# Weight conversion of a folded attention and two-layer network: sign bit through a leaky activation, half of layer two's weight sums by accumulating DMAs, four operand sets instead of five

## The chip, the cores and the metric

The kernel runs on one core of a Trainium2 chip. The metric is the device time of one execution in microseconds (us); less is better. TensorE (PE) does the matrix products, VectorE (DVE) and ScalarE (ACT) work on rows of 128 partitions, GpSimd (POOL) and SyncE (SP) issue DMAs here; a DMA that adds to its target is issued from POOL.

## What is computed

```python
def _attn_ref(q, k, v, tau):
    qn = q / (np.linalg.norm(q, axis=1, keepdims=True) + 1e-06)
    kn = k / (np.linalg.norm(k, axis=1, keepdims=True) + 1e-06)
    s = kn.transpose(0, 2, 1) @ qn / tau
    a = softmax(s)                      # 256 x 256
    return v @ a
def _moe_ref(x, w_in, w_out):           # layer 1
    h = x @ w_in
    return (h * (1.0 / (1.0 + np.exp(-1.702 * h)))) @ w_out
def _moe2_ref(x, w_in, w_out):          # layer 2
    h = x @ w_in
    return np.maximum(0.01 * h, h) @ w_out
```

There are 6016 tokens, 256 channels and 2048 hidden columns. The attention is one over channels, so its 256x256 matrix is multiplied into layer one's first weights once (the "fold"), and the tokens of `v` go straight into layer one. The four weight matrices arrive as 64-bit floats.

## The kernel before

**Number format.** Each 32-bit operand is split into a rounded high part and a low part (the rest), and each product is three matmuls: high by high, low by high, high by low (`terms`, line 96). ACT usually makes the high part with a copy, DVE the low part with a subtraction.

**Work.** The tokens are six pairs of blocks of 512 (the last pair 448), the hidden columns eight pairs of 128, numbered f. A pass i is one layer for one pair of token blocks: passes 0 to 5 are layer one, 6 to 11 layer two. Pass 0 (`hidden_first`) multiplies the plain way; passes 1 to 3 (`step`) use a Strassen scheme of seven products in place of eight for the first matrix of a layer; passes 4 to 11 (`strassen_step`) use it for both. The scheme multiplies sums of weight blocks by sums of token blocks. A step is one f of one pass. In a step of passes 1 to 3 PE does seven first products in the order A11, S2, A12, S3, S1, S4, A22, into two PSUM banks, and between them eight products with the second weights for the step before (`put`).

**Weight preparation.** For each of the 32 pieces of 128x512 values, `convert` (layer one, pass 0) or `words_of` (layer two, passes 1 to 3) makes 32-bit floats of the two words of each 64-bit one: ACT multiplies the high words, read as floats, by a power of two (`scale_words`, 212), DVE shifts the low word (line 242), joins the sign bit to it (247) and then the shifted high word (251). For layer two's pieces, keys `w2i` and `w2o`, one key is begun in each step by `begin_next` at its end. Then three closures follow:

- In the next step `run_casts`, after product S3, lets ACT make the high part of the plain blocks (375 and 376 for `w2i`, where two blocks are also negated; 301 for `w2o`), and the scaling of the key after that.
- At the end of that step `run_due` runs `second`: DVE makes the low part, SP stores both, and DVE makes the four block sums in place (`combine`, 198).
- In the step after that, `run_casts` begins with the high part of the sums (406, "rest" in what follows), and `close`, between DVE's low part of g11 (1140) and its sum into `cc` (1151), runs `third`: low part, store.

The buffer `ta` of a piece is one of two, and so are the buffers `ws` of the split blocks. DVE's sum into `cc` reads the PSUM bank that the next step's first product A11 writes.

**Layer one's sums** (`sums_first`) are made from the folded first weights and the second weights, which take a way through DRAM (`raw1`), eight DVE operations of 128x128 for each f. While `ahead` is set, in pass 0, DVE makes their high parts, later ACT.

**Strassen steps.** Each needs three sets of two buffers for the second products' token operands (`operands`, 1177): g0 in its own step, g1 and g2 in the next one. There are five sets, four of them in the buffers of layer one's second weights and one in `gs`.

Of the kernel before, what the change touches and what calls it, by code (L numbers as in the profile page):

```python
# [7 lines left out]
F32 = mybir.dt.float32  # L8
# [9 lines left out]
def tile_kernel(  # L18
# [28 lines left out]
    nc = tc.nc  # L47
# [32 lines left out]
    x2 = [dram.tile([P, 4, w], F32, name=f"x2{p}") for p, w in enumerate(width)]  # L80
    raw1 = [dram.tile([P, 2, 4, P], F32, name=f"raw1{f}") for f in range(NF)]
    w2a = [dram.tile([P, 7, 2, P], F32, name=f"w2a{f}") for f in range(NF)]
# [44 lines left out]
    with tc.manual_schedule():  # L127
# [28 lines left out]
        def load_piece(key):  # L156
            name, f = key
            if name == "both":
                t = raws[key] = early.tile([P, 2, 4, P], F32, tag="cv", name="cb", bufs=3)
                nc.sync.dma_start(out=t, in_=raw1[f])  # L160
                return
# [35 lines left out]

        def combine(a, turned=False):

            (minus_sum if turned else add)(a[:, 2], a[:, 3], a[:, 2])  # L200
            yield
            subtract(a[:, 3], a[:, 0], a[:, 3])
            yield
            if turned:
                minus_sum(a[:, 0], a[:, 2], a[:, 0])
            else:
                subtract(a[:, 0], a[:, 2], a[:, 0])
            yield
            subtract(a[:, 1], a[:, 1], a[:, 0])
            yield  # L210

        def scale_words(t):

            h = t[:, :, :, 1].bitcast(F32)
            nc.scalar.activation(out=h, in_=h, func=AF.Copy, scale=2.0 ** -112)

# [20 lines left out]
        def bits(key):  # L237

            t = raws[key]
            b = t[:, :, :, 1]  # L240
            a = early.tile([P, 4, P], I32, tag="ta", name="ta", bufs=2)
            nc.vector.tensor_scalar(
                out=a, in0=t[:, :, :, 0], scalar1=29, scalar2=7,
                op0=ALU.logical_shift_right, op1=ALU.bitwise_and,
            )
            yield
            nc.vector.scalar_tensor_tensor(  # L247
                out=a, in0=b, scalar=-0x80000000, in1=a, op0=ALU.bitwise_and, op1=ALU.bitwise_or
            )
            yield  # L250
            nc.vector.scalar_tensor_tensor(
                out=a, in0=b, scalar=3, in1=a, op0=ALU.logical_shift_left, op1=ALU.bitwise_or
            )
            raws.pop(key)
            to_convert.remove(key)
            next_load()
            words_out[key] = a.bitcast(F32)

        def convert(key):
# [10 lines left out]
            if name == "wo":  # L270
                hi, lo = (wo[f][:, s].rearrange("p k c -> p (k c)") for s in range(2))
                for j in range(2):
                    nc.sync.dma_start(
                        out=raw1[f][:, 1, 0::3] if j == 0 else raw1[f][:, 1, 1:3],
                        in_=a[:, 2 * j:2 * j + 2],
                    )
# [26 lines left out]
        def sums_first(f):  # L303
# [9 lines left out]

            yield from combine(t[:, 0])
            high(lambda: wa[f][:, 3:, 0], t[:, 0])
            yield from combine(t[:, 1])
            high(out_blocks, t[:, 1])

            def second():
                subtract(wa[f][:, 3:, 1], t[:, 0], wa[f][:, 3:, 0].bitcast(F32))  # L320
# [3 lines left out]
                subtract(x[:, :, 1], t[:, 1], x[:, :, 0].bitcast(F32))  # L324
                nc.sync.dma_start(out=w1o[f][:, 2:6], in_=x.bitcast(F32))
# [14 lines left out]
        def words_of(key):  # L340
# [30 lines left out]

            if name == "w2i":
                def both_bases():
                    x = kept["x"] = new_blocks(name)
                    nc.scalar.copy(x[:, 0, 0], a[:, 0])
                    nc.scalar.activation(
                        out=x[:, 1:3, 0], in_=a[:, 1:3], func=AF.Copy, scale=-1.0
                    )
                casts.append(both_bases)
            else:  # L380
                high(base_blocks, a[:, some])

            def second():
                x = kept["x"]
                if name == "w2i":
                    subtract(x[:, 0, 1], a[:, 0], x[:, 0, 0].bitcast(F32))
                    minus_sum(x[:, 1:3, 1], a[:, 1:3], x[:, 1:3, 0].bitcast(F32))
                else:
                    subtract(x[:, some, 1], a[:, some], x[:, some, 0].bitcast(F32))
                if name == "w2i":  # L390
                    nc.sync.dma_start(out=dst[:, :3], in_=x[:, :3].bitcast(F32))
                else:
# [23 lines left out]

            due.append(second)

# [359 lines left out]
        fold_half(raw0, 0, 1)  # L778
        nc.sync.dma_start(out=raw1[0][:, 0], in_=raw0)
        folded.add(0)  # L780
# [5 lines left out]
        def fold(f):  # L786
# [11 lines left out]
            nc.sync.dma_start(out=raw1[f][:, 0], in_=raw)  # L798
            folded.add(f)
# [417 lines left out]
        def strassen_step(i, f):  # L1217
# [51 lines left out]
            def first_stage():  # L1269
# [5 lines left out]
                hook("first")  # L1275
                subtract(t13, g[:, 1:3], g[:, 0:2])
                nc.scalar.copy(g1[0], t13)  # L1277
                subtract(t24[:, 0], g[:, 2], t13[:, 0])
                subtract(t24[:, 1], g21, t24[:, 0])
                subtract(g1[1], t13, g1[0].bitcast(F32))  # L1280
# [36 lines left out]
        def begin_drain(i):  # L1317
# [40 lines left out]
            def part_two():  # L1358
                if i == LAST:
                    return  # L1360
                add(to["c"], to["c"], sums[i, M5])
                add(tb, ta, sums[i, M7])

            def join():
                burst(other)
                if i == LAST:
                    add(ta, ta, sums[i, M6])
                    add(tb, ta, sums[i, M7])
                    add(ta, ta, sums[i, M5])
# [62 lines left out]
        def place_v(i, n):  # L1432
            nc.vector.transpose(out=staged_x[i][:, n], in_=vblocks_in.pop(n))

        def cast(to, i, n, j):
            nc.scalar.copy(to[:, 0, n, :width[i % NPAIR]], staged_x[i][:, j])

        def low(to, i, n, j):
            w = width[i % NPAIR]
            subtract(to[:, 1, n, :w], staged_x[i][:, j], to[:, 0, n, :w].bitcast(F32))  # L1440

# [218 lines left out]
```

## Time and profile before

| | us |
|---|---|
| median of 3 runs (lowest, highest) | 1006.01 (1005.89, 1007.33) |
| the profiled execution's own time | 1006.63 |
| its span, first to last instruction | 1004.9 |
| TensorE's granted clock in it, share of full speed | 0.999 |
| PE busy | 997.7 (99%) |
| DVE busy | 881.5 (88%) |
| ACT busy | 760.8 (76%) |
| POOL busy | 21.8 (2%) |
| data moved | 208.36 MB, mean 207 GB/s |

The profiled execution took 1.7 us more than its span, and 0.6 us more than the median. A busy PE is not a PE at its peak, as a matmul's end is modelled; idle time of an engine that others do not wait for costs nothing. In rows of the timeline and the chain the first number is the start in us from the span's start.

### The profile page before, as it was taken

Reading aid. Unit: us, or ns where it says so; the run is one execution under the profiler, and the core shown is the slowest. Engines: PE = TensorE matmul, PEld = TensorE weight load, DVE = VectorE, ACT = ScalarE, POOL = GpSimd, SP = SyncE. Lnnn points to the kernel's source line nnn. Section 1 sums busy time; section 2 is a strip of 40 time slices with the busy share of each in tenths; the row PEclk is TensorE's granted clock in tenths of the full one; section 3 lists DMA queues with packets and bytes.
Section 4 is the critical chain, followed back from the end, with each engine's and each line's share of the span. In section 5 each row is a group of like instructions: output and inputs, shape, how many; then the busy total and the mean of one; then the engine's idle time right before and its main releaser. Section 6 shows DMA issues by size and latency. Waiting matters only on the chain.

```text
span 1004.9 us, 13108 instructions
## 1 busy us (share of the span) xinstructions
PE 997.7 (99%) x4448; PEld 824.6 (82%) x4448; DVE 881.5 (88%) x1304; ACT 760.8 (76%) x1221; POOL 21.8 (2%) x31
## 2 busy tenths in 40 slices
PE   9999999999999999999999999999999999999998
PEld 8888887887888888877998887887887887788897
DVE  7899977878887887999898998998998998998986
ACT  7775557787878787886887886886886897797683
POOL 0000000000000000000000000000000000000000
PEclk9999999999999999999999999999999999999999
DMA  9866477745546753764976775875875875785662
GB/s 347 271 178 183 153 236 247 249 174 189 158 152 195 228 177 84 255 211 139 308 242 218 263 227 168 240 237 180 248 225 193 219 234 188 211 260 178 177 205 48
DMA packets 161619, 208.36 MB, mean 207 GB/s; under 512 B 100624, under 2 KB 126736, under 8 KB 160400
## 3 DMA queue, kind: packets, MB, share of 16 engines
q1 hardware_dynamic: 153808, 200.38, 61.4%
q0 software_dynamic: 3456, 6.16, 3.7%
q10 hardware_dynamic: 4288, 0.98, 0.5%
q8 instruction: 35, 0.57, 0.2%
q14 instruction: 32, 0.26, 0.1%
HBM read 161.87 MB, written 45.61 MB: 206 GB/s over the span
## 4 chain that ended last, share of the span: by engine, by line
PE 97%; DMA 1%; DVE 1%; issue 0%; ACT 0%; ACTq 0%; SPq 0%; DVEq 0%
PE h L100 53%; PE y L841 18%; PE y L100 17%; PE y L1340 5%; PE y L565 3%; DMA qk<-in_k_dram 1%; PE h L712 1%; PE h L841 0%; PE y L712 0%; DVE cc L107 0%; ACTq L498 0%; PE y L670 0%; DVE ta L107 0%; PE h L585 0%; DVE ta L247 0%
## 5 line engine op out<-in xcount | busy, mean ns | idle before, releaser
L100 PE MATMUL h<-xa,wi 128*128 128x512 f32 (+1 forms) x765 | 201.9, 385 | 0.0
L100 PE MATMUL y<-g,wo 128*128 128x512 f32 (+1 forms) x744 | 198.5, 389 | 0.4 <-issue 0.4
L100 PEld LDWEIGHTS h<-xa,wi 128*128 128x128 f32 x765 | 141.5, 188 | 29.7 <-ACT tv L1233 3.3
L100 PEld LDWEIGHTS y<-g,wo 128*128 128x128 f32 x744 | 139.6, 188 | 29.2 <-issue 4.5
L100 PE MATMUL h<-xb,wi 128*128 128x512 f32 (+1 forms) x573 | 152.8, 391 | 0.0
L107 DVE TENSOR_TENSOR g<-t,g 128x1024 fp32r<-128x1024 f32 (+1 forms) x124 | 147.4, 1189 | 0.0
L100 PEld LDWEIGHTS h<-xb,wi 128*128 128x128 f32 x573 | 106.9, 188 | 24.5 <-issue 3.2
L841 PE MATMUL y<-gd,wo 128*128 128x512 f32 (+1 forms) x498 | 124.2, 388 | 0.0
L841 PEld LDWEIGHTS y<-gd,wo 128*128 128x128 f32 x498 | 93.1, 188 | 18.7
L100 PE MATMUL h<-xa,wa 128*128 128x512 f32 x384 | 104.2, 390 | 0.1
L100 PE MATMUL h<-g,wo 128*128 128x512 f32 (+1 forms) x372 | 102.7, 384 | 0.0
L811 ACT ACTIVATE g<-g 128x512 f32<-128x512 f32 (+1 forms) x92 | 57.8, 628 | 44.3 <-DVE g L107 43.3
L100 PE MATMUL h<-xb,wa 128*128 128x512 f32 x312 | 83.9, 391 | 0.7 <-DVE xb L104 0.5
L100 PEld LDWEIGHTS h<-xa,wa 128*128 128x128 f32 x384 | 71.5, 188 | 15.4 <-DVE cc L107 0.5
L100 PEld LDWEIGHTS h<-g,wo 128*128 128x128 f32 x372 | 69.8, 188 | 12.7
L841 PE MATMUL y<-g,wo 128*128 128x512 f32 (+1 forms) x297 | 79.1, 388 | 0.0
L1277 ACT CAST g<-t 128x1024 fp32r<-128x1024 f32 (+1 forms) x62 | 63.8, 1029 | 19.5 <-DVE t L107 18.3
L107 DVE TENSOR_TENSOR g<-g,g 128x1024 fp32r<-128x1024 f32 (+1 forms) x62 | 73.9, 1192 | 0.3
L107 DVE TENSOR_TENSOR t<-g 128x1024 f32<-128x1024 f32 (+1 forms) x62 | 73.2, 1181 | 0.0
L100 PEld LDWEIGHTS h<-xb,wa 128*128 128x128 f32 x312 | 58.3, 188 | 14.0 <-DVE xb L104 1.0
L107 DVE TENSOR_TENSOR g<-tt,h 128x512 f32<-128x512 f32 (+1 forms) x62 | 41.7, 672 | 31.2 <-ACT tt L1241 26.9
L1248 ACT CAST g<-g 128x1024 fp32r<-128x1024 f32 (+1 forms) x62 | 63.7, 1027 | 2.0
(192 smaller groups left out, 1525.6 us busy)
## 6 DMA issues: line engine op xcount, KB each, us to landing
wi<-w2a SPq DMA_DIRECT2D x48, 896.0 KB, 5.5
wo<-w2o SPq DMA_DIRECT2D x46, 768.0 KB, 4.2
wi<-w1a SPq DMA_DIRECT2D x16, 896.0 KB, 6.3
wo<-w1o SPq DMA_DIRECT2D x16, 768.0 KB, 4.8
cv<-in_moe_w_in_dram SPq DMA_DIRECT2D x32, 256.0 KB, 3.4
w1a<-wa SPq DMA_DIRECT2D x8, 896.0 KB, 3.6
stg<-x SPq DMA_DIRECT2D x5, 1024.0 KB, 4.8
stg<-x POOLq DMA_DIRECT2D x20, 256.0 KB, 4.3
```

The source lines that it names most:

```text
L100: nc.tensor.matmul(dst, lhsT=w, rhs=x, start=start, stop=stop, skip_group_check=more)
L107: nc.vector.tensor_tensor(out=out, in0=in0, in1=in1, op=op)
L565: nc.tensor.matmul(s_ps[h][:, :C], lhsT=t[:, 1, r, h * P:(h + 1) * P], rhs=t[:, 0, r, :], start=(j == 0 and r == 0), stop=(j == last and r ...
L712: nc.tensor.matmul(pw, lhsT=e[:, d, c0], rhs=wi[:, x, d], start=i == 0, stop=i == len(todo) - 1)
L811: nc.scalar.activation(out=out, in_=in_, func=AF.Prelu, alpha=0.01)
L841: nc.tensor.matmul(ys[key][kc], lhsT=ws[x], rhs=y, start=first and n == 0, stop=closing or (final and n == 2), skip_group_check=closing,)
L1248: nc.scalar.copy(g0[0], g[:, 0::2])
L1277: nc.scalar.copy(g1[0], t13)
L1340: nc.tensor.matmul(sums[i, M1], lhsT=x, rhs=y, start=False, stop=True, skip_group_check=True,)
```

## The change

- **Sign bit.** ACT's scaling becomes a leaky activation with slope 2^32 for negative values: their exponent then has a bit that DVE's shift by three moves into the sign. DVE's operation of line 247 goes, for all 32 pieces.
- **Pass 0.** The high parts of the first weights (line 284) and of the folded ones (796) go from DVE to ACT. `raw1` has another layout, so that layer one's sums are four operations of 128x256 instead of eight of 128x128.
- **Layer two's sums.** Signs are turned so that `w2i`'s plain blocks are no longer negated; the token operands B21, T4 and T2 of layer two and some of its sums get the other sign instead, in operations that were there before. Of the four sums DVE makes two; the other two are DMAs from POOL that add one 128x128 block of `ta` to another, the second of them reading what the first wrote.
- **Order.** `second` now runs in `close`, before DVE's sum into `cc`; `rest` stays in the next step's `run_casts` and reads what the DMAs added; `third` runs in that step's `run_due`.
- **Operand sets.** Four instead of five.

```diff
         def scale_words(t):
             h = t[:, :, :, 1].bitcast(F32)
-            nc.scalar.activation(out=h, in_=h, func=AF.Copy, scale=2.0 ** -112)
+            nc.scalar.activation(out=h, in_=h, func=AF.Prelu, scale=2.0 ** -112, alpha=2.0 ** 32)
...
-            nc.vector.scalar_tensor_tensor(
-                out=a, in0=b, scalar=-0x80000000, in1=a, op0=ALU.bitwise_and, op1=ALU.bitwise_or
-            )
             yield
...
-                (nc.scalar.copy if f == 0 else nc.vector.tensor_copy)(wi[:, 0], flat)
+                nc.scalar.copy(wi[:, 0], flat)
...
-            yield from combine(t[:, 0])
-            high(lambda: wa[f][:, 3:, 0], t[:, 0])
-            yield from combine(t[:, 1])
-            high(out_blocks, t[:, 1])
+            yield from combine(t)
+            high(lambda: wa[f][:, 3:, 0], t[:, :, 0])
+            high(out_blocks, t[:, :, 1])
...
-                for _ in combine(a, name == "w2i"):
-                    pass
-                casts.insert(0, lambda: nc.scalar.copy(rest_blocks(), a))
-                closing.append(third)
+                minus_sum(a[:, 2], a[:, 3], a[:, 2])
+                subtract(a[:, 3], a[:, 0], a[:, 3])
+                for to, n in ((0, 2), (1, 0)):
+                    nc.gpsimd.dma_start(out=a[:, to], in_=a[:, n], accum_op=ALU.add)
+                casts.insert(0, rest)
+
+            def rest():
+                nc.scalar.copy(rest_blocks(), a)
+                due.append(third)
...
-            due.append(second)
+            closing.append(second)
...
-            nc.vector.tensor_copy(hi, raw)
+            nc.scalar.copy(hi, raw)
             subtract(lo, raw, hi.bitcast(F32))
...
-        sets = [(4 - 3 * (NF * (LAST - FIRST) + REST - 1)) % 5]
+        sets = [0]
         def operands(name):
-            i = sets[0] % 5
+            i = sets[0] % 4
             sets[0] += 1
-            if i == 4:
-                return [late.tile([P, 2, BLK], F32R, tag="gs", name=name, bufs=2) for _ in range(2)]
...
+                if layer == 1:
+                    subtract(t13, g[:, 1:3], g[:, 0:2])
+                    nc.scalar.copy(g1[0], t13)
+                    subtract(t24[:, 0], g[:, 2], t13[:, 0])
+                    subtract(t24[:, 1], g21, t24[:, 0])
+                else:
+                    subtract(t13, g[:, 0:2], g[:, 1:3])
+                    nc.scalar.copy(g1[0], t13)
+                    minus_sum(t24[:, 0], t13[:, 0], g[:, 2])
+                    add(t24[:, 1], g21, t24[:, 0])
```

How DVE's work stands in a step of passes 1 to 3 that finishes a `w2i` key's plain blocks; before, from the end of `close` on (`ta` is the piece, `cv` the words of the next key):

```order
L107 TENSOR_TENSOR w2os<-ta,w2os 128x4x128
L107 TENSOR_TENSOR cc<-tv,h_2408 128x512
L107 TENSOR_TENSOR g_2452<-tt,g_2452 128x512
L107 TENSOR_TENSOR w2i<-ta,w2i 128x128
L113 SCALAR_TENSOR_TENSOR w2i<-ta,w2i 128x2x128
L113 SCALAR_TENSOR_TENSOR ta<-ta 128x128
L107 TENSOR_TENSOR ta<-ta 128x128
L113 SCALAR_TENSOR_TENSOR ta<-ta 128x128
L107 TENSOR_TENSOR ta<-ta 128x128
L242 TENSOR_SCALAR ta<-cv 128x512
L247 SCALAR_TENSOR_TENSOR ta<-cv,ta 128x512
L251 SCALAR_TENSOR_TENSOR ta<-cv,ta 128x512
```

And now, from the low part of g11 on:

```order
L107 TENSOR_TENSOR g_2432<-tp,g_2432 128x512
L107 TENSOR_TENSOR w2i<-ta,w2i 128x3x128
L113 SCALAR_TENSOR_TENSOR ta<-ta 128x128
L107 TENSOR_TENSOR ta<-ta 128x128
L107 TENSOR_TENSOR cc<-tv,h_2390 128x512
L107 TENSOR_TENSOR g_2433<-tt,g_2433 128x512
L107 TENSOR_TENSOR w2os<-ta,w2os 128x4x128
L239 TENSOR_SCALAR ta<-cv 128x512
L245 SCALAR_TENSOR_TENSOR ta<-cv,ta 128x512
```

The key's low part and two sums stand ahead of `cc` now, where the earlier key's low part of the sums (`w2os`) stood, and that one has gone behind g22; five operations for a `w2i` key have gone, four for a `w2o` one.

ACT in the middle of such a step, before: `rest` of the earlier key, the scaling, the plain blocks of a `w2i` key, then the high part of g11 (`g_2637`) and what follows it.

```order
L1131 COPY tt<-h_2595 128x512
L406 CAST w2os<-ta 128x4x128
L215 ACTIVATE cv<-cv 128x512
L375 CAST w2i<-ta 128x128
L376 ACTIVATE w2i<-ta 128x2x128
L1139 CAST g_2637<-tp 128x512
```

And now (g11 is `g_2432`):

```order
L1116 COPY tt<-h_2391 128x512
L391 CAST w2os<-ta 128x4x128
L212 ACTIVATE cv<-cv 128x512
L295 CAST w2i<-ta 128x3x128
L1124 CAST g_2432<-tp 128x512
```

`rest` has kept its place ahead of g11; two operations for a `w2i` key's plain blocks have become one. POOL, which had issued nothing in passes 1 to 3, now stands so (the rows before are the same without the third):

```order
masks.py:199 ISA
masks.py:199 AFFINE_SELECT ident<-ident 128x128
L387 DMA ta<-ta 128x128 x32
L1484 DMA stg<-x_65 128x512 x4
L1484 DMA stg<-x_66 128x512 x4
```

32 accumulating DMAs, two for each of 16 keys, have come ahead of layer two's; PE's order is the same in both kernels.

## Rows read from the trace of the kernel before

**Rows 1.** The profile's first part: busy us, share of the span, by engine.

```profile
PE 997.7 (99%) x4448; PEld 824.6 (82%) x4448; DVE 881.5 (88%) x1304; ACT 760.8 (76%) x1221; POOL 21.8 (2%) x31
```

**Rows 2.** The chain that ended last: share of the span by engine.

```profile
PE 97%; DMA 1%; DVE 1%; issue 0%; ACT 0%; ACTq 0%; SPq 0%; DVEq 0%
```

**Rows 3.** Windows: 25 us of pass 0, busy us by engine, clock.

```profile
100.00:125.00 25.00, 25.00 (x123) 21.14 (x122) 24.21 (x45) 13.59 (x22) 0.00 (x0) 1.00 0.51 158
```

**Rows 4.** Waits of PE, 54 to 400 us: in total, times, longest.

```profile
PE h L100 <- DVE xb L104: 0.5, 1, 0.5
...
PE h L100 <- DVE tt L107: 0.2, 1, 0.2
```

**Rows 5.** Tile `ta` (a piece's 32-bit words): duration in ns, least/median/most.

```profile
L247 DVE SCALAR_TENSOR_TENSOR ta<-cv,ta x32: 681/693/696, 42.4 to 371.8; 128x512 int32<-128x512 int32 x32
...
L107 DVE TENSOR_TENSOR ta<-ta x48: 286/292/294, 214.8 to 380.3; 128x128 f32<-128x128 f32 x48
...
L113 DVE SCALAR_TENSOR_TENSOR ta<-ta x16: 291/293/294, 214.5 to 370.2; 128x128 f32<-128x128 f32 x16
...
L284 DVE CAST wi<-ta x7: 422/427/429, 57.7 to 109.2; 128x512 fp32r<-128x512 f32 x7
```

**Rows 6.** Tile `cv`: ACT's scaling, in ns least/median/most.

```profile
L215 ACT ACTIVATE cv<-cv x32: 657/670/702, 38.2 to 364.8; 128x512 f32<-128x512 f32 x32
```

**Rows 7.** The page's costliest groups: layer two's leaky activation (busy us, mean ns).

```profile
L811 ACT ACTIVATE g<-g 128x512 f32<-128x512 f32 (+1 forms) x92 | 57.8, 628 | 44.3 <-DVE g L107 43.3
```

**Rows 8.** The chain in order of time: start, us, what; in pass 4.

```profile
410.91 3.40 PE h L100 x15
```

**Rows 9.** Timeline where passes 1 and 2 meet: start, us, [idle before].

```profile
228.35 1.89 DVE L104 TENSOR_TENSOR xb<-stg,xb 128x512 fp32r<-128x512 f32 x3
...
229.09 0.50 PE L100 MATMUL h<-xb,wa 128*128 128x512 f32 x1 [0.53 <-DVE xb L104]
...
239.32 0.32 SPq L880 DMA_DIRECT2D x<-stg  x1
```

**Rows 10.** Timeline of one step of pass 2, and the next step's rest.

```profile
262.10 0.62 ACT L406 CAST w2is<-ta 128x512 fp32r<-128x512 f32 x1
...
263.18 0.52 ACT L301 CAST w2o<-ta 128x384 fp32r<-128x384 f32 x1
...
264.25 0.69 DVE L107 TENSOR_TENSOR g<-tp,g 128x512 fp32r<-128x512 f32 x1 [1.08 <-ACT g L1139]
...
264.86 0.69 DVE L107 TENSOR_TENSOR w2is<-ta,w2is 128x512 fp32r<-128x512 f32 x1
...
265.46 0.68 DVE L107 TENSOR_TENSOR cc<-tv,h 128x512 f32<-128x512 f32 x1
...
266.66 0.55 DVE L107 TENSOR_TENSOR w2o<-ta,w2o 128x384 fp32r<-128x384 f32 x1
...
266.85 0.84 PE L100 MATMUL h<-xa,wa 128*128 128x512 f32 x3
...
267.25 1.27 DVE L107 TENSOR_TENSOR ta<-ta 128x128 f32<-128x128 f32 x4
...
272.30 0.62 ACT L406 CAST w2os<-ta 128x512 fp32r<-128x512 f32 x1
```

**Rows 11.** DMA issues: times, KB each, median us to landing.

```profile
stg<-x POOLq DMA_DIRECT2D x20, 256.0 KB, 4.3
...
x<-stg SPq DMA_DIRECT2D x4, 1024.0 KB, 4.7
...
w2o<-w2o SPq DMA_DIRECT2D x10, 256.0 KB, 2.4
...
w2r<-wr SPq DMA_DIRECT2D x4, 64.0 KB, 2.1
```

**Rows 12.** POOL's accumulating DMAs of passes 7 to 11 (tile `stg`).

```profile
L1487 POOL DMA_DIRECT2D stg<-x x24: 865/865/1013, 490.9 to 907.1; - x24
...
DMA to landing us min/median/max: 3.6/4.3/8.4
```

More of the change, by code (lines that the diff above doesn't have):

```diff
@@ L80, in tile_kernel @@
     x2 = [dram.tile([P, 4, w], F32, name=f"x2{p}") for p, w in enumerate(width)]
-    raw1 = [dram.tile([P, 2, 4, P], F32, name=f"raw1{f}") for f in range(NF)]
+    raw1 = [dram.tile([P, 4, 2, P], F32, name=f"raw1{f}") for f in range(NF)]
     w2a = [dram.tile([P, 7, 2, P], F32, name=f"w2a{f}") for f in range(NF)]
@@ L158, in load_piece @@
             if name == "both":
-                t = raws[key] = early.tile([P, 2, 4, P], F32, tag="cv", name="cb", bufs=3)
+                t = raws[key] = early.tile([P, 4, 2, P], F32, tag="cv", name="cb", bufs=3)
                 nc.sync.dma_start(out=t, in_=raw1[f])
@@ L196, in next_load, with combine @@
                     return
-        def combine(a, turned=False):
-            (minus_sum if turned else add)(a[:, 2], a[:, 3], a[:, 2])
+        def combine(a):
+            add(a[:, 2], a[:, 3], a[:, 2])
             yield
@@ L203, in combine @@
             yield
[L204 to L207, printed above, removed]
+            subtract(a[:, 0], a[:, 2], a[:, 0])
             yield
@@ L273, in convert @@
                     nc.sync.dma_start(
-                        out=raw1[f][:, 1, 0::3] if j == 0 else raw1[f][:, 1, 1:3],
+                        out=raw1[f][:, 0::3, 1] if j == 0 else raw1[f][:, 1:3, 1],
                         in_=a[:, 2 * j:2 * j + 2],
@@ L312, in out_blocks @@
                 return kept["x"][:, :, 0]
-            yield from combine(t[:, 0])
-            high(lambda: wa[f][:, 3:, 0], t[:, 0])
-            yield from combine(t[:, 1])
-            high(out_blocks, t[:, 1])
+            yield from combine(t)
+            high(lambda: wa[f][:, 3:, 0], t[:, :, 0])
+            high(out_blocks, t[:, :, 1])
             def second():
-                subtract(wa[f][:, 3:, 1], t[:, 0], wa[f][:, 3:, 0].bitcast(F32))
+                subtract(wa[f][:, 3:, 1], t[:, :, 0], wa[f][:, 3:, 0].bitcast(F32))
                 combined.add(f)
@@ L323, in second @@
                 x = kept["x"]
-                subtract(x[:, :, 1], t[:, 1], x[:, :, 0].bitcast(F32))
+                subtract(x[:, :, 1], t[:, :, 1], x[:, :, 0].bitcast(F32))
                 nc.sync.dma_start(out=w1o[f][:, 2:6], in_=x.bitcast(F32))
@@ L370, in rest_blocks @@
                 return kept["y"][:, :, 0]
[L372 to L381, printed above, removed]
+            high(base_blocks, a[:, some])
             def second():
                 x = kept["x"]
[L385 to L389, printed above, removed]
+                subtract(x[:, some, 1], a[:, some], x[:, some, 0].bitcast(F32))
                 if name == "w2i":
@@ L778, in tile_kernel @@
         fold_half(raw0, 0, 1)
-        nc.sync.dma_start(out=raw1[0][:, 0], in_=raw0)
+        nc.sync.dma_start(out=raw1[0][:, :, 0], in_=raw0)
         folded.add(0)
@@ L795, in fold @@
             hi, lo = wa[f][:, :4, 0], wa[f][:, :4, 1]
-            nc.vector.tensor_copy(hi, raw)
+            nc.scalar.copy(hi, raw)
             subtract(lo, raw, hi.bitcast(F32))
-            nc.sync.dma_start(out=raw1[f][:, 0], in_=raw)
+            nc.sync.dma_start(out=raw1[f][:, :, 0], in_=raw)
             folded.add(f)
@@ L1275, in first_stage @@
                 hook("first")
[L1276 to L1279, printed above, removed]
+                if layer == 1:
[8 more added lines that the diff above has]
+                    add(t24[:, 1], g21, t24[:, 0])
                 subtract(g1[1], t13, g1[0].bitcast(F32))
@@ L1361, in part_two @@
                 add(to["c"], to["c"], sums[i, M5])
-                add(tb, ta, sums[i, M7])
+                (add if layer == 1 else subtract)(tb, ta, sums[i, M7])
             def join():
@@ L1367, in join @@
                     add(ta, ta, sums[i, M6])
-                    add(tb, ta, sums[i, M7])
+                    subtract(tb, ta, sums[i, M7])
                     add(ta, ta, sums[i, M5])
@@ L1433, in place_v, with turned @@
             nc.vector.transpose(out=staged_x[i][:, n], in_=vblocks_in.pop(n))
+        def turned(to, i, n):
+            return i >= NPAIR and (n in (B21, T4) if to is xbt else n == T2)
         def cast(to, i, n, j):
-            nc.scalar.copy(to[:, 0, n, :width[i % NPAIR]], staged_x[i][:, j])
+            hi, raw = to[:, 0, n, :width[i % NPAIR]], staged_x[i][:, j]
+            if turned(to, i, n):
+                nc.scalar.activation(out=hi, in_=raw, func=AF.Copy, scale=-1.0)
+            else:
+                nc.scalar.copy(hi, raw)
         def low(to, i, n, j):
             w = width[i % NPAIR]
-            subtract(to[:, 1, n, :w], staged_x[i][:, j], to[:, 0, n, :w].bitcast(F32))
+            hi, lo = (to[:, x, n, :w] for x in range(2))
+            (minus_sum if turned(to, i, n) else subtract)(lo, staged_x[i][:, j], hi.bitcast(F32))
         def between(i, f):
```

## The prediction

> **What bounds the kernel now.** I read the shares of the engines first: PE is busy for 99% of the span, DVE for 88%, ACT for 76%, POOL for 2% [rows 1]. The chain that ended last then says whose time this is: 97% of it is PE [rows 2]. So I looked for what PE waits for in passes 0 to 3, where nearly all of the change lies: from 54 to 400 us there are two entries, 0.5 and 0.2 us [rows 4]. DVE is almost as full as PE in pass 0, 24.21 of 25 us against ACT's 13.59, and still PE never stops in that window [rows 3]. A lighter DVE can thus return at most these 0.7 us there; what the change can cost is decided by new waits on ACT and DVE that reach PE.
>
> **Sign bit, pass 0, Strassen steps: nothing.** DVE loses 32 operations of 0.693 us, 22.2 us in all, and 7 casts of 0.427 us [rows 5], with as many of the folded weights; they lay beside a PE that did not wait. ACT gets these casts, 14 of about 0.6 us, 9 us over some 100 us in which it is idle for nearly half [rows 3]; if that cover were gone, PE would wait for ACT's high parts, at most those 9 us. The leaky activation runs on ACT at 628 ns for 512 columns in layer two [rows 7], the scaling now takes 670 [rows 6], so their exchange is free; ACT's order has the same three table loads. A subtraction and a negated sum cost DVE the same by size: 0.292 and 0.293 us for 128 columns [rows 5], so the turned signs of layer two cost nothing. PE's order is unchanged.
>
> Four operand sets: g0 now goes into the buffers that g2 of two steps earlier had, whose last reader is M4. PE issues that product before S3 and S1, six matmuls. Fifteen matmuls take 3.40 us [rows 8], so six take 1.36; after them DVE adds (0.68, as for `cc` [rows 10]) and ACT applies the activation (0.63 [rows 7]) before it writes g0. The buffers are free 2.7 us early. I take nothing.
>
> **Where passes meet: -0.5 us.** At 229.09 PE waits 0.53 us for DVE's low parts of xb [rows 9]. Ahead of these on DVE stood four block sums (1.27 us for four, [rows 10]) and the sign operation (0.69, [rows 5]); both have gone there. The 0.2 us wait is PE waiting for a sum of its own product and stays.
>
> **Layer two's sums: the chain that decides.** For 16 keys DVE's 64 block sums become 32 and 32 accumulating DMAs; the 9.3 us (32 by 0.292) saved are covered as above. The new part is a wait: `rest`, in ACT's queue ahead of g11, needs both DMAs landed, and behind it stand the scaling, the plain blocks, g11's high part, then on DVE g11's low part, and the sum into `cc` that PE's next A11 waits for.
>
> How much time the pair has, from one step [rows 10]: DVE's low part of g11 starts at 264.25, the next operation at 264.86. The changed order puts there a low part of 384 columns (0.55) and two sums of 0.29, each starting about 0.03 behind the one before: the second sum ends near 266.05, POOL can issue at 266.1, and the next step's `rest` stands at 272.30. The pair has 6.2 us. `cc` starts at 266.06 in place of 265.46 and ends at 266.74, and A11 starts at 266.85: 0.1 us of slack. A pair that is late by x therefore stops PE for about x less 0.1 us; nothing else in the step absorbs it.
>
> What a pair takes: no row shows an accumulating DMA of 64 KB inside SBUF. Bounds are a plain 64 KB store from SP, 2.1 us from issue to landing [rows 11], and POOL's accumulating DMA of 256 KB, 4.3 in the median and 3.6 at least [rows 12]. It is nearest to the second kind, with a quarter of the bytes; the plain stores of 256 and 64 KB differ by 0.3 us [rows 11], and an accumulation also reads its target, so I take twice that off the quickest one: 3.0 us, an estimate. The second DMA waits for the first, so a pair takes 6.0 us and some 0.1 of semaphores: just in time, for nothing. With the bounds it is 4.3 or 8.7 us.
>
> By the Trainium skill's page "DMA: Bandwidth & Descriptors" (Anatomy of one DMA) a DMA issued from POOL takes about 2.0 us and its bytes over 436 GB/s, so an estimated 2.15 us for 64 KB and 4.4 for a pair. By that rule no pair would be late and the time would be that of the first rival below. The trace disagrees where it can be checked: the rule gives 2.6 us for 256 KB, the rows give 4.3.
>
> Two kinds of key are late all the same. (a) The last two `w2o` keys have 512 columns of plain blocks (0.69 us) and a copy to a raw tile (about 0.25): `cc` comes 0.4 later, 0.3 past the slack, twice: **+0.6**. (b) Where passes 1 and 2, and 2 and 3, meet, the 1 MB store of a pass's output is issued; before at 239.32 [rows 9], now by my count near 238.7, as DVE's copies stand behind less. In that step the second accumulate is issued at about the same time. The store takes 4.7 us where 64 KB take 2.1 [rows 11], so it moves data for 2.6 us; shared evenly, the small transfer comes some 1.3 us later, 1.1 past both slacks, twice: **+2.2**.
>
> **Sum.** -0.5 + 0.6 + 2.2 = +2.3 us. On the profiled execution's 1006.63 us (span 1004.9 and 1.7 around it) that gives 1008.9; this execution was 0.6 us over the median, so on the median of 1006.01 I say **1008.3 us**. A measurement of this kernel can tell about 0.2%, 2.0 us, from no change.
>
> **Rivals.**
> - *All pairs land in time.* For it: plain stores of 384 to 512 KB beside these steps take little longer than 64 KB, and 2.1 is a row. Then only the -0.5 and perhaps part of the 0.6 are left: 1005.5 to 1006.1, not slower. It decides below 2.4 us for one accumulate, as then 1.3 us of contention fit into 6.2. Faster by over 0.2% it is only if passes 0 to 3 hide waits that the trace does not name.
> - *Most pairs are late.* For it: the 256 KB accumulates reach 8.4 us [rows 12] where larger transfers run, and a pair here meets the store of plain blocks, the store of the earlier key's sums and the load of the key after. At 3.3 us for one a pair is late by 0.5, at 3.6 by 1.1. As each late `rest` also delays the next pair's issue, the loss comes again in each of some 15 steps: +7.5 or +16.5, so with the -0.5 1013 to 1022. At the far bound of 4.3 it would be 2.5 per step and 1043; that needs four times the bytes, and I leave it out.
> - A second rule works that way. POOL was busy for 865 ns in nearly all of 24 issues [rows 12], whatever DVE did. The skill's page "SBUF — State Buffer" (SBUF: two separate sides) says that descriptors of a POOL DMA cannot be written while DVE runs an operation that takes both its ports, such as a 32-bit copy. By it the 0.4 us shift of the next key's low words can push the second accumulate back by an estimated 0.4, which is 0.3 late, some 4 us over the 15 steps. The rows bear no sign of it, as none of the 24 is stretched by more than 0.15 us; it is part of this rival's chance.
> - *The change does not do as it says.* ACT now makes the first weights' high parts and waits for DVE's words there; or the write into a reused set waits for PE after all, at 0.2 us in each of some 60 steps 12 us. Nothing in the rows speaks for either; 1006 to 1018.
>
> **How the numbers follow.** The forecast has a chance of 0.40; its own range is 1006.5 to 1010, two thirds of it over the 1008.0 at which slower by 0.2% begins: 0.25 slower, 0.15 within. All in time: 0.30, of which 0.25 within and 0.05 faster. Most late: 0.22, slower. The last: 0.08, 0.05 slower and 0.03 within. Together: faster 0.05, within 0.2% 0.43, slower 0.52. The range runs from 1004.9, which leaves out most of the faster part, to 1015, which leaves out the worse half of "most late": about 0.18 is outside. The likeliest time stays 1008.3.
>
> **What would show it.** POOL has 32 more issues between about 195 and 350 us, with their time to landing under tile `ta`: 3.0 us in the median, and over 4 in two places. ACT's `rest` shows no wait in most steps, and over 1 us in those after 239 and after 320. PE's idle time in passes 1 to 3 is then named after DVE's `cc`, and the 0.53 us at 229 is gone. The words of layer two are done some four steps earlier, as in pass 0 more of layer one's sums are made; DVE's busy time falls by about 40 us and ACT's rises by some 5, with no effect. I am wrong if the accumulates land in 2.4 us or less (then nothing is lost), if they take 3.3 or more (then every step pays), or if PE shows new waits in pass 0 or after 400 us.

## The result, and the profile after

The changed kernel takes 1018.17 us (median of 4 runs, 1016.48 to 1019.86) against 1006.16 for the kernel before, measured beside it: a ratio of 1.0115, 95% interval 1.0103 to 1.0128. It is slower by 12 us. The forecast was 1008.3 and its range ended at 1015.

The page of the changed kernel, shares of the engines and the chain that ended last (its own time is 1019.86 us, 13.2 over the profiled execution before):

```profile
span 1018.1 us, 13055 instructions
...
PE 1001.3 (98%) x4448; PEld 824.0 (81%) x4448; DVE 844.3 (83%) x1190; ACT 766.8 (75%) x1223; POOL 49.2 (5%) x63
...
PE 63%; DMA 1%; DVE 0%; issue 0%; ACT 0%; ACTq 0%
PE h L100 39%; PE y L100 16%; PE y L1329 5%; PE y L826 3%; DMA ta<-ta 1%; PE h L826 0%; DVE cc L107 0%; DVE w2o L107 0%; DVE o L1400 0%; ACT w2o L295 0%; ACT g L1124 0%; DVE ta L113 0%; DVE wr L382 0%; DVE ta L107 0%; ACT w2is L391 0%
```

DVE lost 37 us and ACT gained 6, about as counted, and no time came of it [rows 1]. By the trace a `w2i` key has lost four DVE operations and a `w2o` key three, one fewer each than the section on the change says. What is new is in the chain: `DMA ta<-ta`, one of the new accumulating DMAs, with `DVE cc` and ACT's casts behind it, where there was nearly nothing but PE [rows 2]. The shares here add up to some 64%, as this view follows the chain back only to the accumulate issued at 361.84; PE's 63% is not to be set against the 97% before.

The waits of the changed kernel from 54 to 400 us (engine, line, what it waited for, us in total, times, longest; line numbers above 480 are some 15 lower than before), against two entries before [rows 4]:

```profile
PE h L100 <- DVE cc L107: 9.0, 6, 2.9
ACT w2is L391 <- DMA ta<-ta: 7.2, 4, 3.1
...
ACT w2os L391 <- DMA ta<-ta: 5.0, 3, 1.9
...
PE h L100 <- ACT h L1103: 0.3, 1, 0.3
...
PE h L100 <- DVE tt L107: 0.2, 1, 0.2
```

L391 is `rest`. It waited for a DMA in 7 of 16 keys and not at all in the other 9; six times PE then waited for `cc`. The entry of 0.5 us for `xb` is gone.

PE's order is the same in both kernels, so their matmuls can be set side by side one by one. How far the changed kernel is behind, and where that grows (us; the times in the first column are those of the changed kernel):

```
up to 222     +0.22
227 to 232    -0.38   (a new wait of 0.27, and 0.68 less at 229)
249.4         +4.82   (3.04 of wait, the rest slow matmuls behind it)
272.0         +0.65
283.8         +1.54
317.1         +0.57
347.4         +1.75
359.4         +1.75
371.5         +1.96
after 400     +0.34
sum           13.22
```

Six places, all but those near 230 and 317, stand behind a `cc` that a late `rest` held up; they make 12.5 of it. The first, read row by row (timeline of the changed kernel; start, length, engine, line, operation, out<-in, and in brackets the idle time and what ended it):

```profile
237.14 0.34 SPq L397 DMA_DIRECT2D w2o<-w2os  x1
...
238.37 0.32 SPq L865 DMA_DIRECT2D x<-stg  x1
238.50 0.86 POOL L387 DMA_DIRECT2D ta<-ta  x1 [1.79 <-DVE stg L859]
...
239.39 2.33 SPq L182 DMA_DIRECT2D cv<-in_moe_w_in_dram  x2
...
244.78 0.62 ACT L391 CAST w2is<-ta 128x512 fp32r<-128x512 f32 x1 [3.10 <-DMA ta<-ta]
245.31 0.65 ACT L212 ACTIVATE cv<-cv 128x512 f32<-128x512 f32 x1
245.86 0.50 ACT L295 CAST w2o<-ta 128x384 fp32r<-128x384 f32 x1
246.26 0.61 ACT L1124 CAST g<-tp 128x512 fp32r<-128x512 f32 x1
...
246.91 0.69 DVE L107 TENSOR_TENSOR g<-tp,g 128x512 fp32r<-128x512 f32 x1 [4.38 <-ACT g L1124]
...
247.51 0.55 DVE L107 TENSOR_TENSOR w2o<-ta,w2o 128x384 fp32r<-128x384 f32 x1
...
248.10 0.29 DVE L113 SCALAR_TENSOR_TENSOR ta<-ta 128x128 f32<-128x128 f32 x1
...
248.43 0.29 DVE L107 TENSOR_TENSOR ta<-ta 128x128 f32<-128x128 f32 x1
...
248.64 0.68 DVE L107 TENSOR_TENSOR cc<-tv,h 128x512 f32<-128x512 f32 x1
...
249.38 0.50 PE L100 MATMUL h<-xa,wa 128*128 128x512 f32 x1 [2.88 <-DVE cc L107]
```

The 1 MB store is issued 0.13 us ahead of the key's second accumulate. That lands some 6 us behind its issue, `rest` stands 3.10 us, and the wait runs down the chain that the prediction named: scaling, plain blocks, g11's high part on ACT, its low part on DVE, the two sums, `cc`, and PE's A11 2.9 us late. Behind it matmuls are slow for a while. The trace in windows (length, busy time of each engine, granted clock, DMA share, GB/s):

```profile
246.30:249.40 3.10, 0.22 (x2) 0.03 (x1) 2.42 (x6) 2.27 (x6) 0.15 (x1) 1.00 0.11 39
250.60:253.70 3.10, 3.10 (x9) 2.41 (x9) 3.07 (x5) 1.54 (x2) 0.86 (x1) 0.55 0.75 206
```

From 250.6 to 253.7 the granted clock is 0.55, nearly all of it the lower level of 1.2 GHz, and a matmul of 512 columns starts 0.43 us behind the one before in place of 0.227: eight of them cost 1.6 us more.

### The profile page after: what moved, and what is told of

Read it like the earlier page. It is cut to its first block, busy times and chain, and to the rows that moved or that the text cites. A ratio compares the mean times of both kernels' runs of the same rounds, so it can differ in the third digit from the quotient of the medians.

```text
span 1018.1 us, 13055 instructions
## 1 busy us (share of the span) xinstructions
PE 1001.3 (98%) x4448; PEld 824.0 (81%) x4448; DVE 844.3 (83%) x1190; ACT 766.8 (75%) x1223; POOL 49.2 (5%) x63
## 4 chain that ended last, share of the span: by engine, by line
PE 63%; DMA 1%; DVE 0%; issue 0%; ACT 0%; ACTq 0%
PE h L100 39%; PE y L100 16%; PE y L1329 5%; PE y L826 3%; DMA ta<-ta 1%; PE h L826 0%; DVE cc L107 0%; DVE w2o L107 0%; DVE o L1400 0%; ACT w2o L295 0%; ACT g L1124 0%; DVE ta L113 0%; DVE wr L382 0%; DVE ta L107 0%; ACT w2is L391 0%
## 5 line engine op out<-in xcount | busy, mean ns | idle before, releaser
L100 PEld LDWEIGHTS y<-g,wo 128*128 128x128 f32 x744 | 139.6, 188 | 29.2 <-issue 4.5
L826 PEld LDWEIGHTS y<-g,wo 128*128 128x128 f32 x297 | 56.6, 190 | 12.0
```

The source lines that it names most:

```text
L100: nc.tensor.matmul(dst, lhsT=w, rhs=x, start=start, stop=stop, skip_group_check=more)
L826: nc.tensor.matmul(ys[key][kc], lhsT=ws[x], rhs=y, start=first and n == 0, stop=closing or (final and n == 2), skip_group_check=closing,)
```

## Experiments

Two theories stood at the start. **A**: a key's pair of accumulates is late where other transfers are ahead of it, and `rest`, in front of g11 on ACT, hands that to PE. **B**: the change of order alone does it, two sums and a wider low part ahead of `cc` on DVE and more casts on ACT.

**1. Both sums back on DVE, behind `cc`.**

```
-                for to, n in ((0, 2), (1, 0)):
-                    nc.gpsimd.dma_start(out=a[:, to], in_=a[:, n], accum_op=ALU.add)
+                due.append(last_sums_of)
...
+            def last_sums_of():
+                for to, n in ((0, 2), (1, 0)):
+                    add(a[:, to], a[:, to], a[:, n])
```

> The changed kernel, but with its two accumulating DMAs put back as two sums on DVE behind cc; sign bit, pass 0, four operand sets, turned signs and the place of the other two sums stay as changed. Theory A (late pairs: in 7 of 16 keys the second accumulate lands late, rest holds ACT, so g11, cc and PE are late): all of the loss is gone, 1005.3 to 1006.5 us, and from 54 to 400 us PE waits for DVE's cc less than 0.6 us in all against 9.0. Theory B (DVE's new order: a low part of 384 columns and two sums now stand ahead of cc, and ACT has more casts): these stay, so the time stays at 1015 to 1019.

Measured: 1007.35 us against 1006.41 beside it, ratio 1.0009 (1.0000 to 1.0019). PE's waits for anything on another engine:

```profile
PE h L100 <- ACT h L1106: 0.3, 1, 0.3
PE h L100 <- DVE tt L107: 0.2, 1, 0.2
```

All waits for `cc` are gone, and 10.8 of the 12 us with them, so the accumulates cost that and theory B falls for the bulk. It is not wholly wrong: the time is 0.85 above the bound I gave, and the matmuls set side by side still show a wait of 0.27 us at 228 and one of 0.47 at 310, where passes meet, without a DMA to wait for.

**2. One accumulate**, the second sum on DVE just ahead of `rest`.

```
-                for to, n in ((0, 2), (1, 0)):
-                    nc.gpsimd.dma_start(out=a[:, to], in_=a[:, n], accum_op=ALU.add)
+                nc.gpsimd.dma_start(out=a[:, 0], in_=a[:, 2], accum_op=ALU.add)
...
             def rest():
+                add(a[:, 1], a[:, 1], a[:, 0])
```

> The changed kernel with one accumulating DMA: the second sum is done by DVE just before ACT's rest. Theory A with the pair as the unit: one DMA has all of some 6 us, and the slowest one seen took 6.2 us to land beside the 1 MB store; no step is late by more than 0.5 us, 1005.5 to 1007 us. A variant, A2 (any accumulate beside other transfers is late, one or two): the three or four worst places stay, 1009 to 1014. Theory B: 1015 to 1019.

Measured: 1007.24 us, ratio 1.0006 (0.9997 to 1.0016); 0.24 over the bound, with the same two waits of 0.27 and 0.47. The 16 accumulates took 2.4 us to land in the median and 3.7 at most, and none was waited for. One accumulate has room enough; it takes a pair to be late, and the second of a pair is issued where stores and loads are.

**3. `rest` later**: both accumulates kept, and `rest` put behind g22's high part in ACT's order.

```
-                casts.insert(0, rest)
+                resting.append(rest)
...
             nc.scalar.copy(g22[:, 0], tt)
+            run_resting()
```

> The changed kernel, both accumulating DMAs kept, but ACT's rest stands behind the high part of g22 in place of ahead of the scaling and g11. Theory A: the pair has some 3 us more (scaling 0.65, plain blocks 0.50, g11 0.61, activation 0.63, g22 0.62), and a late rest holds neither g11 nor cc; only the step beside the 1 MB store can still be late, by about 0.1 to 0.5, so 1005.5 to 1007 us, though the DMAs land just as late as before. Theory B: 1015 to 1019. If a late rest only moves the wait (to DVE's third, in front of the next step): 1008 to 1015.

Measured: 1005.53 us, ratio 0.9991 (0.9982 to 1.0000). PE's waits from 54 to 400 us, and the time of the 32 accumulates to landing:

```profile
PE y L100 <- issue: 0.4, 1, 0.4
PE h L100 <- DVE tt L107: 0.2, 1, 0.2
```

```profile
L387 POOL DMA_DIRECT2D ta<-ta x32: 859/862/1015, 194.0 to 359.9; - x32
...
DMA to landing us min/median/max: 2.3/2.6/5.9
```

The DMAs are as slow as in the changed kernel (there 2.3, 2.5 and 6.2), and nobody pays: what cost 12.6 us was where their reader stands. Both waits where passes meet went too, so with the new order of DVE's work they needed `rest` ahead of g11.

**4. The three 1 MB stores of a pass's output issued later**, behind the next key's loads.

```
-                    nc.sync.dma_start(out=x2[p], in_=staging(("y", p))[:, :, :w])
+                    behind.append(lambda: nc.sync.dma_start(out=x2[p], in_=y2))
...
             begin_next()
+            while behind:
+                behind.pop()()
```

> The changed kernel, with the three 1 MB stores of a pass's output issued behind the next key's loads of words, 1 to 1.5 us later, so that the second accumulate is issued ahead of the store. Theory A with other transfers as the cause of a late landing: the wait of 3.0 us at 246 and the 1.7 us of matmuls at half the granted clock behind it go, at most 0.5 us of wait stays there: 1013 to 1014.5 if the later waits stay as they are; as their places hang on when each load falls, 1010 to 1015.5. If the pair is late by its own length, whatever runs beside it: 1017 to 1019.

Measured: 1018.23 us, ratio 1.0118 (1.0103 to 1.0133): by the total, a miss. The matmuls side by side show why. The wait near 246 and its slow matmuls are gone, 4.8 us; but at 345 a wait of 3.5 us stands where the changed kernel has 1.6, and those at 268 and 280 grew a little. Ahead of the wait at 345 the third store is issued at 325.17 and the 896 KB load of layer one's weights right behind it; the load now lands 3.4 us behind the next pair's first issue, in place of 1.4 in the changed kernel, and that first accumulate takes 4.8 us to land in place of 3.9. The total alone could not tell this from "the pair is late by its own length".

**5. The kernel of run 3 again**, as the reference for runs 6 and 7.

> The kernel with rest behind g22's high part, once more, as the reference of the next two runs on one chip: 1005.2 to 1005.9 us, ratio to the kernel before 0.9985 to 0.9998.

Measured: 1005.76 us, ratio 0.9994 (0.9985 to 1.0003).

**6. `rest` later and both sums on DVE** (the edits of runs 1 and 3 together).

> The kernel with rest behind g22's high part, with both accumulating DMAs put back as sums on DVE behind cc. If the two accumulates give nothing even where they land in time (DVE's 32 sums of 0.29 us lie beside PE): the same as the kernel with rest later, within 0.5 us, 1005.2 to 1006.0. If DVE's 9 us less are what made that kernel faster: 1006.2 us or more. That the two waits of 0.27 and 0.47 us where passes meet go as well (they stood in the run with both sums on DVE, with no DMA to wait for) would show that ACT's order made them.

Measured: 1005.81 us, ratio 0.9996 (0.9987 to 1.0005). The same as run 5, so the accumulates give nothing even when they are in time. Against run 1 only the place of `rest` differs, and 1.3 us (by the ratios) and the two waits are gone: that is what ACT's order costs with no DMA in it.

**7. `rest` later, and one DVE operation per key put back.**

```
+            nc.vector.scalar_tensor_tensor(
+                out=a, in0=b, scalar=0, in1=a, op0=ALU.bitwise_and, op1=ALU.bitwise_or
+            )
```

> The kernel with rest behind g22's high part, with one operation of DVE put back per key of words, where the sign operation stood (it is given a zero, so it changes no value): 22 us more of DVE work in all. If the gain where passes 1 and 2 meet comes from the sign operation having left DVE's queue there: PE's wait of about 0.5 us at 229 comes back and the time is 0.4 to 0.8 us over the kernel with rest later, 1005.9 to 1006.5. If it comes from elsewhere (the place of the sums): no wait there, 1005.2 to 1005.9.

Measured: 1005.98 us, ratio 0.9997 (0.9988 to 1.0006). DVE has 865.9 us of work in place of 844.7 in run 5, and PE pays nothing; the wait at 229 does not come back. In run 6 the sign operation is gone but two sums stand there again, and the wait is gone as well. So it goes when the four sums leave that place, and also when two sums and the sign operation do; which single operation would be enough was not tried.

**8. Plain copies in place of accumulating ones.**

```
-                    nc.gpsimd.dma_start(out=a[:, to], in_=a[:, n], accum_op=ALU.add)
+                    nc.gpsimd.dma_start(out=a[:, to], in_=a[:, n])
```

> The changed kernel with its 32 accumulating DMAs as plain copies of the same 64 KB, from the same queue at the same places (it leaves out the last two sums of layer two's weights). If reading the target is what a DMA here pays for (as the prediction's estimate of 3.0 us has it): an undisturbed copy lands 0.3 us or more below the 2.3 us of the accumulate, the pairs get 0.6 us more, and the time falls to 1008 to 1014. If the queue of other transfers decides: the same landing within 0.15 us, the same late places, 1016 to 1019.5.

Measured: 1012.46 us, ratio 1.0061 (1.0047 to 1.0075). The accumulates of the changed kernel first, the copies of this run below (duration of POOL's instruction, min/median/max in ns; landing in us):

```profile
L387 POOL DMA_DIRECT2D ta<-ta x32: 859/859/1012, 194.1 to 374.3; - x32
...
DMA to landing us min/median/max: 2.3/2.5/6.2
```

```profile
L387 POOL DMA_DIRECT2D ta<-ta x32: 534/534/711, 193.8 to 366.8; - x32
...
DMA to landing us min/median/max: 1.8/2.2/5.3
...
PE h L100 <- DVE cc L107: 4.0, 4, 1.5
```

By its numbers the first expectation holds: undisturbed, the first copy of a pair lands in 1.8 us in place of 2.3, the second in 2.2, and a pair takes 4.3 us in place of 5.0; half of the loss goes. That reading the target is what costs is not shown: of the first copy's 0.5 us, 0.32 pass ahead of its first packet (1.11 us behind the issue in place of 1.43), about as much as POOL's instruction is shorter. And most of the gain comes of the order of issues again: near 246 PE falls 0.5 us behind in place of 4.8, as the second copy there is issued 0.46 us ahead of the 1 MB store and not behind it. The other places beside other transfers stay (5.3 us to landing at most), so both matter: the pair's own length takes the spare time, and the traffic does the rest.

**9. One 1 MB store later**, the one near 238 us alone.

```
+                    if p == 1:
+                        behind.append(lambda: nc.sync.dma_start(out=x2[p], in_=y2))
...
```

> The changed kernel with one 1 MB store alone moved: the one near 238 us is issued behind the next key's loads, the one near 326 stays where the change has it (in the run with all three stores moved, the wait near 246 and its slow matmuls went, and a wait of 3.5 us came near 342, where the change has 1.6). If each late pair is set by the transfers issued just ahead of its second accumulate: 3.0 us and the 1.7 of matmuls at half the granted clock go, some 0.3 come back in the next two waits, 1013 to 1014.5 us. If what is taken from one pair always comes back at another: 1016.5 to 1019.

Measured: 1014.45 us, ratio 1.0078 (1.0063 to 1.0093): 3.7 us below the changed kernel, at the upper end of what was expected. PE waits 5.8 us for `cc` in place of 9.0, 1.6 at the longest. What is taken from one pair does not always come back.

**10. The store of the four sums issued twice.**

```
-                nc.sync.dma_start(
+                for _ in range(2):
+                    nc.sync.dma_start(
```

> The changed kernel with the 512 KB store of each key's four sums issued twice (the second writes the same values): more traffic, issued some 1.3 us behind the next key's first accumulate. If traffic ahead of the second accumulate makes it late: its data then lasts until some 4.5 us behind the first issue where the second accumulate's packets want to start at 4.05, the spare time is 0.85 us, and most of the 16 pairs become late by up to 1.5: 1022 to 1032 us. If only the few large transfers (1 MB store, loads of layer one's weights) matter: 1017 to 1020.

Measured: 1018.56 us, ratio 1.0117 (1.0100 to 1.0134). The expectation fell, and the edit did not do what I meant. One key in the timeline of this run, then the same key in the changed kernel:

```profile
257.17 0.86 POOL L387 DMA_DIRECT2D ta<-ta  x1 [6.71 <-ACT cc L795]
...
258.47 3.01 SPq L398 DMA_DIRECT2D w2o<-w2os  x2
...
260.09 0.86 POOL L387 DMA_DIRECT2D ta<-ta  x1 [2.06 <-DMA ta<-ta]
...
261.57 1.27 SPq L182 DMA_DIRECT2D cv<-in_moe_w_in_dram  x2
...
262.89 0.62 ACT L391 CAST w2is<-ta 128x512 fp32r<-128x512 f32 x1
```

```profile
261.04 0.86 POOL L387 DMA_DIRECT2D ta<-ta  x1 [8.28 <-ACT cc L794]
...
262.34 0.34 SPq L397 DMA_DIRECT2D w2o<-w2os  x1
...
263.53 1.20 SPq L182 DMA_DIRECT2D cv<-in_moe_w_in_dram  x2
263.66 0.86 POOL L387 DMA_DIRECT2D ta<-ta  x1 [1.76 <-DVE ta L245]
...
267.42 0.62 ACT L391 CAST w2is<-ta 128x512 fp32r<-128x512 f32 x1 [0.53 <-DMA ta<-ta]
```

The second store writes where the first wrote, so SP waits some 2.7 us for the first to land, and all that stands behind it in SP's queue comes later: the loads of words now follow the second accumulate by 1.48 us, and `rest` does not wait. PE waits for `cc` in 4 places in place of 6, 5.6 us; one of them, of 3.2, has again slow matmuls behind it, and the total comes out the same by chance. So this is a second test of what stands ahead of an accumulate; whether more bytes ahead of it make it later was not tried.

**11. Three accumulates.** DVE's subtraction for the fourth block also becomes a DMA, and a sum of no use stands in its place on DVE.

```
-                subtract(a[:, 3], a[:, 0], a[:, 3])
-                for to, n in ((0, 2), (1, 0)):
+                minus_sum(a[:, 3], a[:, 3], a[:, 3])
+                for to, n in ((3, 0), (0, 2), (1, 0)):
```

> The changed kernel with a third accumulating DMA in the chain of each key, for the subtraction of DVE (a meaningless sum of the same size stands in its place on DVE, so the values are not the reference's). An undisturbed accumulate delays the next by 2.62 us and rest stands 5.85 us behind the first issue, so every one of the 16 keys is late by about 1.75, and those beside other transfers by more: 15 steps of 1.7 and some 7 us, 1030 to 1045 us. If rest had more room than that and traffic alone decided: 1017 to 1025.

Measured: 1059.99 us, ratio 1.0531 (1.0516 to 1.0547). Waits from 54 to 430 us, then two windows around the first late key:

```profile
PE h L100 <- DVE cc L107: 33.5, 14, 5.6
...
ACT w2is L391 <- DMA ta<-ta: 25.3, 8, 5.6
...
ACT w2os L391 <- DMA ta<-ta: 12.9, 7, 3.2
```

```profile
204.00:207.60 3.60, 0.68 (x4) 0.22 (x2) 2.29 (x7) 2.89 (x7) 0.34 (x1) 0.97 0.09 31
207.60:210.70 3.10, 3.08 (x7) 2.48 (x8) 3.07 (x6) 2.48 (x4) 1.10 (x2) 0.50 0.76 237
```

The room was right: `rest` waits in all 16 keys, 15 times for the accumulates by name and once, 3.5 us, by name for a load of v; where nothing large runs beside them PE mostly stops for 1.3 to 2.0 us a key (1.7 expected). The time is 15 us over the range, and that is the clock: set side by side, PE's waits sum to some 37 us, and matmuls at half the granted clock behind the longer ones to some 15 more, which I had left out.

## Why the prediction was wrong

*What bounds the kernel; sign bit, pass 0, four sets.* Right. PE is all that counts, new waits in pass 0 or after 400 us did not come, and runs 5 and 7 show that 21 us of DVE work more or less change nothing.

*-0.5 where passes meet.* Right in itself: 0.68 us went at 229 us. But `cc`, later by the new order, passes its lateness to ACT's casts of xb, and PE waits 0.27 and 0.5 us where passes 1 and 2, and 2 and 3, meet (in run 1 they stand without any DMA, in run 6, with `rest` later, they are gone). The sum of this term is about zero.

*The pair has 6.2 us.* Nearly: in the key above `rest` would have stood at 266.89, 5.85 us behind POOL's first issue. What is missing is POOL: I had it issue 0.05 us behind the sum's end, and it does so 0.53 us behind it in 15 of the 16 keys (0.59 in the first).

*One accumulate 3.0 us.* Too long. Undisturbed it lands in 2.3 us, the second is issued 2.62 behind the first, and a pair takes 5.0 us. So an ordinary key has 0.85 us to spare, not nothing, and 9 of 16 keys paid nothing. The prediction said that nothing is lost if an accumulate lands in 2.4 us or less. It did land so, and 12 us were lost: that sign counted on 1.3 us of contention at the most. By the Trainium skill's rule that was weighed there (page "DMA: Bandwidth & Descriptors", Anatomy of one DMA), an estimated 2.15 us, the small transfer is priced better than by my rows of 256 KB; between its two measured kinds, 1.8 for a copy and 2.3 for an accumulate, it makes no difference.

*+0.6 for the last two `w2o` keys.* Hardly seen: with the sums on DVE (run 1) PE falls 0.2 us behind at the first of them, at 339, and not at the second.

*+2.2 for two collisions.* **This is the step that failed**, as "shared evenly, the small transfer comes some 1.3 us later, 1.1 past both slacks, twice". One of the two places was right, and its size wrong: near 246 it is 3.0 of wait and 1.6 to 1.8 of slow matmuls (run 9 gave back 3.7 in the median of its runs). The other collision did not come. Where passes 2 and 3 meet, no key is begun (`if f < NF - 1 or i == 1`, ahead of `begin_next`), so no accumulate is issued between 317.01 and 334.82, and the store there has landed 4.3 us behind its issue:

```profile
326.39 0.34 SPq L865 DMA_DIRECT2D x<-stg  x1
...
334.82 0.86 POOL L387 DMA_DIRECT2D ta<-ta  x1 [16.95 <-ACT cc L794]
```

The transfers are not shared evenly. In the trace's packets the store's 128 packets of 8 KB go out from 239.3 to about 242, at 325 ns each on 16 engines, and the accumulate's first packet, due 1.43 us behind its issue, moves 3.46 behind it, when nearly all of these are through. By the Trainium skill (page "DMA: Bandwidth & Descriptors", Queues, rings and completion order) a DMA engine empties a whole packet of descriptors of one queue before it turns to the next. The trace agrees in that the store's 128 pieces, 8 for each of 16 engines if they share alike, went nearly all ahead of the accumulate, and no run here shows how many such a packet may hold. Then the words' loads, issued behind the accumulate, share with its last packets, which go 5.8 us behind the issue in place of 2.0.

And the count was short: I looked for 1 MB stores alone. Late pairs stand behind loads of words (one issued 0.13 us ahead of the second accumulate at 263.66), behind loads of v, and behind the loads of layer one's next weights, 768 and 896 KB, issued 0.9 and 1.2 us ahead of the second accumulates at 361.84 and 350.23. Five places of the six, 7.7 us, were not in the sum.

In two late pairs the first accumulate is late already, with 3.9 us to landing, and the second is issued 4.2 us behind it in place of 2.62. The earlier of the two, and the queue of the page that stands in its way:

```profile
271.91 0.86 POOL L387 DMA_DIRECT2D ta<-ta  x1 [7.39 <-ACT cc L794]
...
276.12 0.86 POOL L387 DMA_DIRECT2D ta<-ta  x1 [3.35 <-DMA ta<-ta]
```

```profile
q8 instruction: 35, 0.57, 0.2%
```

This queue moves 35 packets of 16 KB, none of them issued by the kernel's own DMAs. One of them runs from 273.19 to 274.62. Of the accumulate's 128 packets 120 have gone out by 273.9, and the last eight, a sixteenth, start at 274.60. The same stands at this key in runs 2, 3, 4, 9 and 10, and in run 8 with 15 of 16 packets: the last sixteenth starts within 0.02 us of the end of such a packet, and the DMA takes 3.6 to 4.0 us. In the runs among them where `rest` stands ahead of g11 and a key has two DMAs (4, 8, 9, 10), PE falls 1.5 to 1.7 us behind at this key whatever was moved elsewhere, against 1.5 in the changed kernel. That one DMA engine of 16 was held by that packet fits this; the trace does not name the engine of a packet.

The rival *most pairs are late* gave the right time for a reason that is only half right: 7 of 16 pairs were late, by traffic, and not each by the accumulates' own length. That its range of 1013 to 1022 held the measured time is in part luck.

*The second rule (both ports).* No sign of it again: POOL was busy for 859 ns in the median and at most 1012 of 32 issues.

Left out altogether was the price of a long wait in slow matmuls. Open is one thing: that each of the other five places would go if the transfer ahead of it were moved is argued from the order of the issues and packets; moving one transfer alone was tried for one store (run 9).

## What to carry to other kernels

A sum moved to a DMA takes the time that the traffic of its worst moment gives it: list every transfer that can be issued shortly ahead of it, on any queue, and do not count on an even share. Here a 1 MB store issued 0.13 us ahead put the landing off by 3.9 us, loads of 768 and 896 KB issued 0.9 to 1.2 us ahead by 2.1 to 3.0. Some transfers, as those of the queue `q8 instruction`, do not stand in the kernel at all. The reader of such a DMA belongs behind the work on its engine that the critical path needs; here five instructions later in ACT's queue were worth 12.6 us, and moving two sums of a key to DMAs was worth nothing (runs 5 and 6). Taking work from an engine that stands beside a full one returned nothing here, so it was not worth a risk: the best version here, with `rest` later, is 0.4 to 0.9 us below the kernel before by its medians (ratios 0.9991 and 0.9994), which these runs do not tell from none.

## What was not expected of the hardware

- An accumulating DMA of 64 KB goes out in 128 packets of 512 bytes, and a plain copy of the same tile from the same queue in 16 of 4 KB. POOL's issue takes 859 ns for the one and 534 for the other, and, undisturbed, the first of a key lands in 2.3 and 1.8 us.
- POOL issues a key's first DMA 0.53 us behind the end of the DVE operation that it waits for (0.59 in the first key), and the second 0.28 to 0.30 us behind the landing of the first.
- The granted clock fell to the lower level in or behind PE's waits of 2.9 us and more: in the changed kernel (2.9), in run 10 (3.2), and at all six of run 11 (2.9 to 5.6), for 7 to 14 matmuls, while at those of 0.4 to 1.7 us it stayed, and of two waits of 1.8 us in run 11 it fell behind one. Length alone does not tell it, though. In run 4 PE waited 3.3 us, and the clock stayed (windows of that run, the wait and the stretch behind it):

```profile
341.90:345.45 3.55, 0.26 (x3) 0.00 (x1) 2.58 (x7) 2.58 (x6) 0.12 (x1) 1.00 0.09 30
345.45:348.60 3.15, 3.15 (x14) 2.61 (x15) 3.08 (x6) 2.24 (x4) 1.07 (x2) 1.00 1.06 319
```

Why it stayed there is open.
